# Another order for layer 2 of the first chunk: a fused attention and MLP kernel on one Trainium2 core

## The chip, the cores and the metric

The kernel runs on one core of one Trainium2 chip. The engines of the core work side by side, each through its own queue and in its own order: TensorE multiplies matrices (the profile's PE, with the loads of its stationary operand shown as PEld), VectorE (DVE) and ScalarE (ACT) work on elements, GpSimd (POOL) casts and issues DMAs, SyncE (SP) issues DMAs only. They wait for each other by semaphores. The metric is the device time of one launch in microseconds, as the median of several runs; lower is better.

## The reference

Eight batches of eight heads, 576 positions, 64 numbers a head. First attention with a causal mask and a bias from a running sum of `s`, then an MLP with the exact GELU over all 8 x 576 = 4608 tokens of width 512:

```
scores = q @ k.T / sqrt(D)
cum    = cumsum(maximum(s, 0))
scores = where(causal, -1e9, scores + minimum(-(cum_i - cum_j), 0))
attn   = softmax(scores)              # sum + 1e-9 below the line
x      = (attn @ v), heads side by side: 4608 x 512
out    = gelu(x @ w_in) @ w_out       # 512 -> 2048 -> 512
```

## The kernel before, in words

**Attention of a batch.** The kernel computes scores transposed, keys on the partitions. The bias is a product: it multiplies v by `wb`, the exponential of the running sum (`scale_v`, VectorE, one instruction for each of five key tiles of 128, the last of 64), and the row factor cancels in the division. `sc_mm(b, p, slots)` computes the scores of head pair p (0 to 3) in two units, each into one PSUM slot, and ScalarE takes the exponential of each unit into the tile P. `mask` multiplies the diagonal blocks by a triangle (VectorE). `av_main(b, qd, ...)` takes pairs qd and qd + 2: TensorE makes a denominator (`av_d`, from P and `wb`) and two products (`av_o`, from P and the scaled v, `vv`); ScalarE makes the reciprocal by a logarithm and an exponential for each half, four steps (`recip`); VectorE multiplies and writes xT, the transposed input of the MLP. `av_tails` does the same for the last 64 positions of all pairs. `squares_v` sums the squares of v on ScalarE, a 128x2048 and a 64x512 activation; the sums serve only a final test of the value range. Its output tile, `junk`, is never read.

**q and k of batches 0, 1 and 2** are loaded by GpSimd (`load_front`, cast on the way to tiles fq and fk) and transposed on TensorE (`tr_one`, one slot; `tr_two`, the banks M0 and M1), then copied to `qkT` by VectorE or ScalarE. From batch 3 on, q and k are loaded as float32 (`load_qk`), cast by GpSimd and transposed by DMA.

**The MLP** runs in nine chunks of 512 tokens; chunk c needs batch c's main part. Layer 1 has eight items (`l1_item(c, f2)`): each fills one PSUM slot with two 512-wide blocks from eight matmuls, and ScalarE takes the GELU of both at once into gT. An item must wait until the GELU of the item that used its slot before is done. Layer 2 of chunk 0 is plain: four subtiles of 128 tokens, 16 matmuls each over the 16 blocks of gT (`l2_item(c, sub, f0, f1)`), a copy to the output tile `o_sb` (one tile for two subtiles) and a store. Subtiles 0 and 1 accumulate in M0 and M1, 2 and 3 in the two halves of a slot. From chunk 1 on, layer 2 uses seven products of half-size blocks (`prod`), with sums of gT (`S`, by `sums_a`) and of w_out (`T1` to `T4`, by `sums_b`) made by VectorE.

**Stages.** While the MLP works on chunk c, the scores and products of batch c + 1 stand in between its layer-2 matmuls. The order on each engine is written out by hand: the schedule is manual, and every engine takes its instructions in the order of the calls. PSUM has eight banks: the slots x, y and z of two banks each, and the single banks M0 and M1. `order[c]` names the slots in the order in which layer 1 of chunk c takes them; for chunk 1, items 2 to 7 take s2, s1, s2, s0, s2, s0.

**Queues.** SyncE issues the loads of v (`load_v`), the stores of the output and the DMA transposes; GpSimd issues the loads of q, k and weights. Requests in a queue go in order. Some are held back by a tiny operation that reads what an earlier DMA wrote: `behind` is a small DMA on SyncE, `behind_v` a one-element copy on GpSimd that reads a tile of v. raw v of batch 1 has its buffer in common with raw k of batch 3; raw v of batches 0 and 2 share another.

ScalarE loads one set of function tables for the exponential and the logarithm (`exp_set`) and another for GELU; each switch is an ACT_TABLE_LOAD.

Of the kernel before, what the change touches and what calls it, by code (L numbers as in the profile page):

```python
# [19 lines left out]
def kernel(  # L20
# [128 lines left out]

    def behind_v(b, st):  # L150

        nc.gpsimd.tensor_copy(seen_v[:, b : b + 1], raws[b, "v"][0:1, st, 0, 0:1])

    wb = const.tile([128, ST, BH], bf16, name="wb")
    xT = work.tile([128, NP, XW], fp16, name="xT")
# [74 lines left out]
            amx[:, b * NP + p], qkT[b % 2][:, :, p, :S], axis=AX, op=ALU.max, apply_absolute_value=True  # L230
        )

    def squares_v(b):
        t = raws[b, "v"]
        n = work.tile([128, (ST - 1) * H * D], bf16, tag="P", bufs=4, name="junk")
        for j, (n_st, st0, st1) in enumerate(((128, 0, ST - 1), (SL, ST - 1, ST))):
            nc.scalar.activation(  # L237
                n[:n_st, : (st1 - st0) * H * D], t[:n_st, st0:st1].rearrange("p s h d -> p (s h d)"),
                func=AF.Square, accum_out=amv[:n_st, b, j : j + 1],
            )  # L240
# [244 lines left out]
            if lo < hi:  # L485
                yield lo, hi, (t0 + lo) % XW

    def av_pe(b, qd, den, two):

        oo = bank(two, [128, 2, 512], fp32, "av_o")  # L490
        o = [oo[:, t] for t in range(2)]
        av_mm(b, qd, den, None, MAIN)
        for t in range(2):
            av_mm(b, qd, o[t], t, MAIN)
        return o

    def av_out(b, qd, den, o):
# [7 lines left out]
                        ln[:, c * 256 + lo : c * 256 + hi], op=MULT,  # L505
                    )

    def av_main(b, qd, one, two):
        den = bank(one, [128, 512], fp32, "av_d")
        o = av_pe(b, qd, den, two)  # L510
        av_out(b, qd, den, o)

    def tails_pe(b, slot):
# [46 lines left out]
            for i in range(2):  # L560
                nc.scalar.activation(gT_of[c][:, f2 * 2 + i, :], h_ps[:, i], func=AF.Gelu)  # L561

    def l2_item(c, sub, f0=0, f1=FT, slot=None, eng=None):

        gT = gT_of[c]
        if f0 == 0:
            if slot is None:
                o_of[c, sub] = bank(M[sub % 2], [128, KO * 128], fp32, "o_ps")
            elif slot in M:
                o_of[c, sub] = bank(slot, [128, KO * 128], fp32, "o_ps")  # L570
            elif sub == 2:
                two = bank(slot, [128, 2, KO * 128], fp32, "o_ps")
                o_of[c, 2], o_of[c, 3] = two[:, 0], two[:, 1]
        o_ps = o_of[c, sub]
        for ft in range(f0, f1):
            nc.tensor.matmul(  # L576
                o_ps, lhsT=gT[:, ft, sub * 128 : (sub + 1) * 128],
                rhs=w_out_r[:, ft], start=(ft == 0), stop=(ft == FT - 1),
            )
        if f1 < FT:  # L580
            return
        if sub % 2 == 0:
            osb_of[0] = two_sb()
        copy(eng or nc.vector, osb_of[0][:, sub % 2], o_ps)
        store(c, 1 + sub // 2, osb_of[0], subs=slice(sub % 2, sub % 2 + 1))
# [315 lines left out]
    for c in range(NCH):  # L901
# [13 lines left out]
        else:  # L915
            l1_item(c, 0, 0, KO - 2)
            l1_item(c, 0, KO - 2)
            l1_item(c, 1)
        if 1 < c:
            transpose_tiles(nb)  # L920
            if nb + 1 < B:
# [6 lines left out]
        for f2 in range(2, FT // 2):  # L928
            l1_item(c, f2, slot=(s2, s1, s2, s0, s2, s0)[f2 - 2] if c == 1 else None)
            if c == 1 and f2 in (2, 4):  # L930
                tr_two(2, f2 // 2 - 1, 0, both)
                tr_one(2, f2 // 2 - 1, 1, nc.vector, (s0, s1)[f2 // 2 - 1])
            if c == 1 and f2 == 3:
                squares_v(1)
                load_qk(3, "k")
            if c == 1 and 3 <= f2 < 5:
                scale_v(2, STS[f2 - 3 : f2 - 2], nc.vector)
            if c == 1 and f2 == 5:
                sums_a(c, (1, 2, 3), 0, HF // 2)
                scale_v(2, STS[2:4], nc.vector)  # L940
                squares_v(2)
            if c > 1 and f2 == 3:
                scale_v(nb, [(0, 4), (4, 5)], nc.vector)
                sums_a(c, (1, 2, 3), 0, HF // 2)
# [7 lines left out]
                    behind(2, raws[nb + 1, "k"][0:1, ST - 2, 0, :])  # L952
                    load_v(nb + 1, [nc.sync])
        if c == 0:
            squares_v(0)
            sums_b((1, 2, 3, 4), 0, 4)
            exp_set()
            x, y, z = order[0]
            l2_item(c, 0, 0, 8)
            l2_item(c, 1, 0, 8)  # L960
            tr_one(1, 0, 0, nc.vector, z)
            tr_one(1, 0, 1, nc.scalar, x)
            l2_item(c, 2, 0, 8, y)
            sc_mm(1, 0, (z, x))
            l2_item(c, 3, 0, 8, y)
            sc_mm(1, 1, (z, x))
            mask(1, 0, nc.vector)
            sums_b((1, 2, 3), 4, 8)
            behind(1, w_out_r[0:1, FT - 5, 0:D])
            load_v(1, [nc.sync])  # L970
            l2_item(c, 0, 8, 12)
            l2_item(c, 1, 8, 12)
            tr_one(1, 1, 0, nc.vector, z)
            tr_one(1, 1, 1, nc.scalar, x)
            mask(1, 1, nc.vector)
# [250 lines left out]
```

## Time and profile before

| | us |
|---|---|
| median of 3 runs (lowest to highest) | 311.64 (311.57 to 312.32) |
| the profiled execution | 312.71 |
| its span, first to last instruction | 310.8 |
| TensorE busy | 291.5 |
| ScalarE busy | 247.1 |
| VectorE busy | 227.4 |
| GpSimd busy | 98.3 |
| mean granted TensorE clock | 0.996 of full |

The profiled execution is one of its own, beside the three timed runs. The profile gives the busy time of each engine, the chain of work that ended last (followed back from the last instruction to what released it), a timeline for each engine, and the busy time in chosen stretches. In a timeline row, the first number is the start from the beginning of the span, the second the length; then come engine, source line, operation, output and input by the program's names with shapes, and the count of instructions merged into the row. Brackets at the end give the idle time of the engine before the row and what ended it. Layer 1 of chunk 0 runs from 22.3 to 36.1, layer 2 of chunk 0 from 36.1 to 58.7, chunk 1 from 58.7 to 93.2.

### The profile page before, as it was taken

To read this page: it belongs to the slowest core of one execution; us is meant where nothing else is said; L and a number is where in the kernel's file an instruction comes from. 1 tells how busy PE (TensorE), PEld (TensorE's weight loads), DVE (VectorE), ACT (ScalarE), POOL (GpSimd) and SP (SyncE) were. 2 spreads that over 40 slices of the span, in tenths; PEclk is the share of its full clock that TensorE was granted. 3 is DMA by queue.
4 is the path that set the end of the run, shared out by engine and by line. 5 is a ranking of instruction groups with operands and counts; after the bars stand their busy time and mean duration, and the time that the engine had idled before them with its cause. 6 is when DMAs were issued, how large, how long until landed. Compare 5 with 4: busy or idle time off the path is not lost.

```text
span 310.8 us, 8463 instructions
## 1 busy us (share of the span) xinstructions
PE 291.5 (94%) x3522; PEld 196.3 (63%) x3522; DVE 227.4 (73%) x428; ACT 247.1 (80%) x348; POOL 98.3 (32%) x180
## 2 busy tenths in 40 slices
PE   0789999999999999999999999999999999999990
PEld 0564444555784578457854785478647886887880
DVE  3697347968879787787875697658797888766860
ACT  3786787879977997899788987898879877967830
POOL 6575007105080467137621953095400000000000
PEclk9999999999999999999999999999999999999998
DMA  7999999996707696969597859967990030021022
GB/s 119 195 189 203 207 179 177 278 229 149 148 15 205 120 221 135 251 114 223 116 257 142 193 116 243 199 156 152 210 223 9 2 138 2 0 96 41 2 70 76
DMA packets 77933, 45.07 MB, mean 145 GB/s; under 512 B 63168, under 2 KB 70336, under 8 KB 77888
## 3 DMA queue, kind: packets, MB, share of 16 engines
q1 hardware_dynamic: 67104, 24.93, 34.3%
q0 software_dynamic: 10784, 19.53, 32.3%
q8 instruction: 29, 0.48, 0.7%
q14 instruction: 16, 0.13, 0.1%
HBM read 36.85 MB, written 9.44 MB: 149 GB/s over the span
## 4 chain that ended last, share of the span: by engine, by line
PE 84%; ACT 6%; DVE 4%; DMA 2%; issue 2%; POOL 0%; ACTq 0%; POOLq 0%
PE h_ps L550 31%; PE o_al L764 17%; PE o_ga L764 9%; PE h_ps L667 6%; PE sc_ps L434 5%; PE o_be L764 4%; PE av_o L463 4%; ACT junk L237 3%; PE av_d L463 2%; DMA fk<-in_k_dram 2%; PE o_ps L576 2%; ACT P L440 2%; DVE vv L247 2%; PE tr_ps L395 1%; PE av_t L463 1%
## 5 line engine op out<-in xcount | busy, mean ns | idle before, releaser
L550 PE MATMUL h_ps<-xT,w_in_r 128*128 128x512 f16 x480 | 105.9, 379 | 0.4 <-ACT gT L558 0.3
L550 PEld LDWEIGHTS <-w_in_r 128*128 128x128 f16 x480 | 46.7, 98 | 54.5 <-issue 0.6
L558 ACT ACTIVATE gT<-h_ps 128x1024 f16<-128x1024 f32 x49 | 49.0, 1018 | 18.6 <-PE h_ps L550 18.5
L440 ACT ACTIVATE P<-sc_ps 128x1024 bf16<-128x1024 f32 x64 | 60.2, 1032 | 3.4 <-PE sc_ps L434 3.3
L764 PEld LDWEIGHTS <-S 128*128 128x128 f16 x512 | 48.3, 98 | 8.3 <-issue 0.9
L229 DVE TENSOR_REDUCE amx<-qkT 128x2 f32<-128x1152 bf16 x32 | 41.6, 1344 | 0.6 <-DMA qkT<-qk_bf 0.6
L764 PEld LDWEIGHTS <-gT 128*128 128x128 f16 x384 | 36.4, 98 | 7.0 <-issue 1.3
L448 DVE TENSOR_TENSOR P<-P,tri_bf 128x512 bf16<-128x512 bf16 x64 | 25.9, 419 | 11.3 <-ACT P L440 10.7
L754 DVE TENSOR_TENSOR S<-gT 128x1024 f16<-128x1024 f16 (+1 forms) x30 | 21.6, 721 | 15.1 <-ACT gT L561 13.1
L764 PE MATMUL o_al<-T,S 128*128 128x256 f16 x256 | 31.7, 273 | 0.0
L197 POOL DMA_DIRECT2D raw_k<-in_k_dram x25 | 21.0, 849 | 15.5 <-ACT junk L237 15.5
L434 PE MATMUL sc_ps<-qkT 64*128 64x256 bf16 (+2 forms) x320 | 22.3, 264 | 3.1 <-DVE qkT L404 1.7
L503 DVE TENSOR_TENSOR xT<-av_o,ln 128x256 f16<-128x256 f32 (+2 forms) x72 | 23.7, 385 | 1.7 <-ACT ln L479 1.0
L247 DVE TENSOR_TENSOR vv<-raw_v,wb 128x512 bf16<-128x512 f32 (+2 forms) x25 | 24.0, 1001 | 0.1
L434 PEld LDWEIGHTS <-qkT 64*128 64x128 bf16 x320 | 13.8, 98 | 12.2 <-issue 6.9
L197 POOL DMA_DIRECT2D raw_q<-in_q_dram x25 | 21.1, 857 | 1.2 <-POOL seen_v L148 1.2
L237 ACT ACTIVATE junk<-raw_v 128x2048 bf16<-128x2048 f32 (+1 forms) x16 | 20.3, 1266 | 0.3
L404 DVE COPY qkT<-tr_ps 128x576 bf16<-128x576 bf16 (+1 forms) x13 | 11.7, 938 | 10.4 <-PE tr_ps L395 10.4
L681 DVE TENSOR_TENSOR k<-h_ps,k 128x512 f32<-128x512 f32 (+1 forms) x12 | 11.3, 955 | 8.1 <-PE h_ps L667 5.5
L479 ACT ACTIVATE ln<-ln,lnb 128x256 f32<-128x256 f32 x32 | 16.3, 508 | 1.0
L463 PEld LDWEIGHTS <-vv 128*32 128x32 bf16 x768 | 16.3, 100 | 0.6 <-DVE vv L247 0.2
L463 PE MATMUL av_o<-P,vv 128*32 128x256 bf16 (+1 forms) x512 | 16.7, 272 | 0.0
(132 smaller groups left out, 424.9 us busy)
## 6 DMA issues: line engine op xcount, KB each, us to landing
raw_v<-in_v_dram SPq DMA_DIRECT2D x32, 256.0 KB, 5.1
out_dram<-o_sb SPq DMA_DIRECT2D x14, 512.0 KB, 3.6
raw_q<-in_q_dram POOLq DMA_DIRECT2D x20, 256.0 KB, 4.8
raw_k<-in_k_dram POOLq DMA_DIRECT2D x20, 256.0 KB, 6.9
w_out_r<-in_moe_w_out_dram POOLq DMA_DIRECT2D x4, 512.0 KB, 12.8
out_dram<-o_sb SPq DMA_DIRECT2D x7, 256.0 KB, 6.9
fq<-in_q_dram POOLq DMA_DIRECT2D x6, 288.0 KB, 6.8
fk<-in_k_dram POOLq DMA_DIRECT2D x6, 288.0 KB, 7.8
```

The lines of the kernel that those rows point to most:

```text
L197: nc.gpsimd.dma_start(out=t[:n_st, st], in_=src)
L229: nc.vector.tensor_reduce(amx[:, b * NP + p], qkT[b % 2][:, :, p, :S], axis=AX, op=ALU.max, apply_absolute_value=True)
L237: nc.scalar.activation(n[:n_st, : (st1 - st0) * H * D], t[:n_st, st0:st1].rearrange("p s h d -> p (s h d)"), func=AF.Square, accum_out=amv ...
L247: eng.tensor_tensor(vb[:n_st, st0:st1, h0:h1, :], t[:n_st, st0:st1, h0:h1, :], wb[:n_st, st0:st1, b * H + h0 : b * H + h1] .unsqueeze(3).t ...
L434: nc.tensor.matmul(s_ps[:, e, off : off + n], lhsT=qkT[b % 2][e * 64 : e * 64 + 64, 1, p, jt * 128 : jt * 128 + 128], rhs=qkT[b % 2][e * 6 ...
L440: nc.scalar.activation(P[:, :, UO[u] : UO[u] + UW[u]], s_ps[:, :, : UW[u]], func=AF.Exp, scale=scale)
L448: eng.tensor_tensor(d, d, tri_bf.unsqueeze(1).unsqueeze(1).to_broadcast([128, 2, 2, 128]), op=MULT)
L463: nc.tensor.matmul(o[g * 32 : g * 32 + 32, lo : lo + n], lhsT=(wb[:, jt, b * H + 2 * g + qd : b * H + 2 * g + qd + 1].to_broadcast([128, 3 ...
L503: nc.vector.tensor_tensor(xT[:, 2 * qd + t, x0 : x0 + hi - lo], o[t][:, c * 256 + lo : c * 256 + hi], ln[:, c * 256 + lo : c * 256 + hi], ...
L550: nc.tensor.matmul(h_ps[:, i, :], lhsT=w_in_r[:, ko, ft * 128 : (ft + 1) * 128], rhs=xT[:, ko, c * NB % XW : c * NB % XW + NB], start=(ko ...
L558: nc.scalar.activation(gT_of[c][:, f2 * 2 : f2 * 2 + 2, :], h_ps, func=AF.Gelu)
L764: nc.tensor.matmul(o[u], lhsT=lhs[:, f, u * 128 : u * 128 + 128], rhs=rhs[:, f], start=start and j == 0 and (by_sub or u == 0), stop=j == ...
```

## The change

All of it lies in chunks 0 and 1 and in batches 0, 1 and 2. The counts of matmuls, activations and bytes stay the same; seven of the eight sums of w_out of 128x1024 become fourteen of 128x512, and the copy on GpSimd is added.

- The squares of v of batch 0 move from behind layer 1 of chunk 0 to between its items 3 and 4. Those of batches 1 and 2 are cut: the 128x2048 part and the 64x512 part are issued apart, in layer 1 of chunk 1.
- In layer 2 of chunk 0, transposes, scores, masks, sums and the scaling of v of batch 1 stand at other places between the matmuls.
- In batch 1, the products come before the denominators (`last=True`).
- The last four matmuls of subtiles 2 and 3 come behind batch 1's tails, and both copies behind these; VectorE copies subtile 2, ScalarE subtile 3. Before, ScalarE copied subtile 2 and VectorE subtile 3.
- The slots of chunk 1 rotate: items 0 and 1 take z and x (before: y and z).
- v of batch 2 is requested ahead of the stores of chunk 0, and a one-element copy on GpSimd that waits for its second tile stands ahead of the request of q of batch 3.

ScalarE at the end of layer 1 of chunk 0 (gT: GELU; junk: squares; qkT: copy of the transposed k; P: exponentials), before and then after:

```order
L558 ACTIVATE gT<-h_ps 128x1024 x7
L561 ACTIVATE gT<-h_ps 128x512 x2
L237 ACTIVATE junk,amv<-raw_v 128x2048
L237 ACTIVATE junk,amv<-raw_v 64x512
L863 ACT_TABLE_LOAD
L402 COPY qkT_119<-tr_ps 128x2x576
```

```order
L558 ACTIVATE gT<-h_ps 128x1024 x4
L238 ACTIVATE junk,amv<-raw_v 128x2048
L238 ACTIVATE junk,amv<-raw_v 64x512
L558 ACTIVATE gT<-h_ps 128x1024 x3
L561 ACTIVATE gT<-h_ps 128x512 x2
L866 ACT_TABLE_LOAD
L403 COPY qkT_119<-tr_ps 128x2x576
```

The two squares moved from ahead of the table load to behind the fourth GELU.

ScalarE from the tails of batch 1 (lnt) into layer 1 of chunk 1, before and then after:

```order
L479 ACTIVATE lnt<-lnt,lnb 128x128
L558 ACT_TABLE_LOAD
L558 ACTIVATE gT<-h_ps 128x1024 x4
L237 ACTIVATE junk,amv<-raw_v 128x2048
L237 ACTIVATE junk,amv<-raw_v 64x512
L558 ACTIVATE gT<-h_ps 128x1024 x2
```

```order
L480 ACTIVATE lnt<-lnt,lnb 128x128
L403 COPY o_sb<-o_ps 128x512
L558 ACT_TABLE_LOAD
L558 ACTIVATE gT<-h_ps 128x1024 x2
L238 ACTIVATE junk,amv<-raw_v 128x2048
L558 ACTIVATE gT<-h_ps 128x1024 x2
L238 ACTIVATE junk,amv<-raw_v 64x512
L558 ACTIVATE gT<-h_ps 128x1024
```

An output copy came in ahead of the table load, and the large square moved up from behind the fourth GELU to behind the second.

SyncE's requests (raw_v: v of batches 1, 2 and 3; out_dram: stores of chunk 0), before and then after:

```order
L225 DMA raw_v<-in_v_dram 128x8x64 x4
L225 DMA raw_v<-in_v_dram 64x8x64
L779 DMA out_dram<-o_sb 128x512 x4
L225 DMA raw_v<-in_v_dram 128x8x64 x4
L225 DMA raw_v<-in_v_dram 64x8x64
```

```order
L225 DMA raw_v<-in_v_dram 128x8x64 x4
L225 DMA raw_v<-in_v_dram 64x8x64
L225 DMA raw_v<-in_v_dram 128x8x64 x4
L225 DMA raw_v<-in_v_dram 64x8x64
L782 DMA out_dram<-o_sb 128x512 x4
```

The four stores moved behind the five loads of v of batch 2.

```diff
-    def squares_v(b):
+    def squares_v(b, js=(0, 1)):
         t = raws[b, "v"]
         n = work.tile([128, (ST - 1) * H * D], bf16, tag="P", bufs=4, name="junk")
-        for j, (n_st, st0, st1) in enumerate(((128, 0, ST - 1), (SL, ST - 1, ST))):
+        for j in js:
+            n_st, st0, st1 = ((128, 0, ST - 1), (SL, ST - 1, ST))[j]
...
-    def av_pe(b, qd, den, two):
+    def av_pe(b, qd, den, two, last=False):
...
-        av_mm(b, qd, den, None, MAIN)
-        for t in range(2):
-            av_mm(b, qd, o[t], t, MAIN)
+        for t in (0, 1, None) if last else (None, 0, 1):
+            av_mm(b, qd, den if t is None else o[t], t, MAIN)
...
-    def l2_item(c, sub, f0=0, f1=FT, slot=None, eng=None):
+    def l2_item(c, sub, f0=0, f1=FT, slot=None, eng=None, out=True):
...
-        if f1 < FT:
-            return
+        if f1 == FT and out:
+            l2_out(c, sub, eng)
+
+    def l2_out(c, sub, eng=None):
+        o_ps = o_of[c, sub]
         if sub % 2 == 0:
             osb_of[0] = two_sb()
         copy(eng or nc.vector, osb_of[0][:, sub % 2], o_ps)
...
+        if c == 1:
+            squares_v(1, (0,))
...
+            if c == 0 and f2 == 3:
+                squares_v(0)
+                sums_b((1, 2, 3, 4), 0, 2)
             if c == 1 and f2 == 3:
-                squares_v(1)
+                squares_v(1, (1,))
                 load_qk(3, "k")
...
+            if c == 1 and f2 == 4:
+                squares_v(2, (0,))
             if c == 1 and f2 == 5:
                 sums_a(c, (1, 2, 3), 0, HF // 2)
                 scale_v(2, STS[2:4], nc.vector)
-                squares_v(2)
+                sums_b((4,), 4, 8)
+                squares_v(2, (1,))
...
         if c == 0:
-            squares_v(0)
-            sums_b((1, 2, 3, 4), 0, 4)
+            sums_b((1, 2, 3, 4), 2, 4)
             exp_set()
             x, y, z = order[0]
             l2_item(c, 0, 0, 8)
-            l2_item(c, 1, 0, 8)
             tr_one(1, 0, 0, nc.vector, z)
             tr_one(1, 0, 1, nc.scalar, x)
+            l2_item(c, 1, 0, 8)
+            sc_mm(1, 0, (z, x))
             l2_item(c, 2, 0, 8, y)
-            sc_mm(1, 0, (z, x))
+            mask(1, 0, nc.vector)
+            sc_mm(1, 1, (z, x))
             l2_item(c, 3, 0, 8, y)
-            sc_mm(1, 1, (z, x))
-            mask(1, 0, nc.vector)
-            sums_b((1, 2, 3), 4, 8)
+            sums_b((1, 2, 3), 4, 6)
             behind(1, w_out_r[0:1, FT - 5, 0:D])
             load_v(1, [nc.sync])
+            tr_one(1, 1, 0, nc.vector, z)
+            tr_one(1, 1, 1, nc.scalar, x)
             l2_item(c, 0, 8, 12)
             l2_item(c, 1, 8, 12)
-            tr_one(1, 1, 0, nc.vector, z)
-            tr_one(1, 1, 1, nc.scalar, x)
             mask(1, 1, nc.vector)
-            sums_b((4,), 4, 8)
             behind_v(1, 1)
             for qd in range(2):
                 for n in "qk":
                     load_front(2, n, qd)
+            sc_mm(1, 2, (z, x))
+            sums_b((1, 2, 3), 6, 8)
+            scale_v(1, STS[0:2], nc.vector)
             l2_item(c, 2, 8, 12)
             l2_item(c, 3, 8, 12)
-            sc_mm(1, 2, (z, x))
-            l2_item(c, 0, 12, eng=nc.scalar)
+            mask(1, 2, nc.vector)
             sc_mm(1, 3, (z, x))
-            mask(1, 2, nc.vector)
-            scale_v(1, STS, nc.vector)
-            l2_item(c, 1, 12, eng=nc.scalar)
-            l2_item(c, 2, 12, eng=nc.scalar)
+            load_v(2, [nc.sync])
+            scale_v(1, STS[2:5], nc.vector)
+            for i in range(2):
+                l2_item(c, i, 12, eng=nc.scalar)
             mask(1, 3, nc.vector)
-            av_main(1, 0, M[0], z)
-            l2_item(c, 3, 12)
-            av_main(1, 1, M[1], x)
+            av_main(1, 0, M[0], z, last=True)
+            av_main(1, 1, M[1], x, last=True)
             av_tails(1, M[0])
-            order[1] = (y, z, x)
-            load_v(2, [nc.sync])
+            l2_item(c, 2, 12, out=False)
+            l2_item(c, 3, 12, out=False)
+            l2_out(c, 2)
+            l2_out(c, 3, nc.scalar)
+            order[1] = (z, x, y)
+            behind_v(2, 1)
             load_qk(3, "q")
```

More of the change, by code (lines that the diff above doesn't have):

```diff
@@ L150, in behind_v @@
     def behind_v(b, st):
-        nc.gpsimd.tensor_copy(seen_v[:, b : b + 1], raws[b, "v"][0:1, st, 0, 0:1])
+        nc.gpsimd.tensor_copy(seen_v[:, b % 2 : b % 2 + 1], raws[b, "v"][0:1, st, 0, 0:1])
     wb = const.tile([128, ST, BH], bf16, name="wb")
@@ L506, in av_out, with av_main @@
                     )
-    def av_main(b, qd, one, two):
+    def av_main(b, qd, one, two, last=False):
         den = bank(one, [128, 512], fp32, "av_d")
-        o = av_pe(b, qd, den, two)
+        o = av_pe(b, qd, den, two, last)
         av_out(b, qd, den, o)
```

## The prediction

> **What bounds it now.** I read the page first, then the chain of work that ended last, then the stretches of the span around the change.
>
> ```profile
> span 310.8 us, 8463 instructions
> ...
> PE 84%; ACT 6%; DVE 4%; DMA 2%; issue 2%; POOL 0%; ACTq 0%; POOLq 0%
> ```
>
> The chain is TensorE for 84% of the span. So a microsecond that TensorE stops waiting is worth a microsecond, as long as nothing later hands it back. What there is to win is seen by comparing a stretch with a quiet one of the same work. Columns: stretch, its length, busy us (and instructions) of TensorE, weight load, VectorE, ScalarE and GpSimd, then clock, DMA share and GB/s.
>
> ```profile
> 36.10:58.70 22.60, 21.79 (x393) 11.41 (x392) 14.00 (x30) 19.05 (x27) 7.22 (x10) 1.00 1.06 192
> 58.70:74.75 16.05, 15.70 (x209) 7.52 (x208) 13.37 (x20) 13.35 (x20) 3.87 (x5) 1.00 0.80 214
> 74.75:83.05 8.30, 7.88 (x89) 5.95 (x88) 5.99 (x13) 8.27 (x11) 0.35 (x1) 1.00 0.72 153
> 93.20:107.00 13.80, 13.80 (x66) 6.26 (x64) 12.94 (x12) 11.26 (x14) 1.82 (x5) 1.00 0.65 160
> 107.00:114.87 7.87, 7.87 (x89) 6.02 (x88) 5.02 (x11) 7.84 (x10) 7.04 (x9) 1.00 0.94 212
> ```
>
> The first row is layer 2 of chunk 0, the second layer 1 of chunk 1, the third the start of its layer 2. The last two are the same two stages of chunk 2, where TensorE has no gap (13.80 and 7.87 busy of as much). The third row is 0.43 longer than the fifth (8.30 - 7.87). The rows of TensorE around the change, with the idle time of the engine and what ended it in brackets:
>
> ```profile
> 40.38 1.90 PE L576 MATMUL o_ps<-w_out_r,gT 128*128 128x512 f16 x8
> 42.51 0.61 PE L434 MATMUL sc_ps<-qkT 64*128 64x256 bf16 x10 [0.23 <-ACT qkT L402]
> 43.06 1.90 PE L576 MATMUL o_ps<-w_out_r,gT 128*128 128x512 f16 x8
> 44.89 0.61 PE L434 MATMUL sc_ps<-qkT 64*128 64x256 bf16 x10
> 45.44 1.90 PE L576 MATMUL o_ps<-w_out_r,gT 128*128 128x512 f16 x8
> ...
> 51.47 0.39 PE L434 MATMUL sc_ps<-qkT 64*128 64x256 bf16 x4
> 52.37 0.40 PE L434 MATMUL sc_ps<-qkT 64*128 64x256 bf16 x6 [0.52 <-ACT P L440]
> ...
> 54.53 0.57 PE L463 MATMUL av_d<-P,wb 128*32 128x256 bf16 x16
> 54.93 1.07 PE L463 MATMUL av_o<-P,vv 128*32 128x256 bf16 x32
> ...
> 57.29 0.94 PE L463 MATMUL av_o<-P,vv 128*32 128x256 bf16 x32
> ...
> 58.70 5.34 PE L550 MATMUL h_ps<-xT,w_in_r 128*128 128x512 f16 x24
> ...
> 64.05 0.76 PE tr_ps L395 x72
> ...
> 71.30 3.61 PE L550 MATMUL h_ps<-xT,w_in_r 128*128 128x512 f16 x16 [0.34 <-ACT gT L558]
> ...
> 80.89 0.40 PE L434 MATMUL sc_ps<-qkT 64*128 64x256 bf16 x6 [0.42 <-ACT P L440]
> ```
>
> Ends are modelled, so I measure from start to start. Eight layer-2 matmuls take 1.83 (43.06 to 44.89), ten score matmuls 0.55 (44.89 to 45.44). Hence four places lose time: 0.30 at 42.51 (due at 42.21), 0.68 at 52.37 (four of ten take 0.22, due at 51.69), 0.13 in the attention product (1.07 against 0.94; it waits for scaled v), and in layer 1 of chunk 1, where the 13.80 of chunk 2 plus two transpose groups of 0.76 would make 15.32, 0.73.
>
> **The change, part by part.** The rows of ScalarE and VectorE from which I price it:
>
> ```profile
> 37.27 1.91 ACT L237 ACTIVATE junk<-raw_v 128x2048 bf16<-128x2048 f32 x1
> ...
> 40.05 1.28 ACT L863 ACT_TABLE_LOAD   x1
> 41.34 1.12 ACT L402 COPY qkT<-tr_ps 128x1152 bf16<-128x1152 bf16 x1
> ...
> 52.83 3.09 DVE L247 TENSOR_TENSOR vv<-raw_v,wb 128x512 bf16<-128x512 f32 x5
> ...
> 57.52 0.39 ACT L478 ACTIVATE ln<-av_d 128x256 f32<-128x256 f32 x1 [0.26 <-PE av_d L463]
> ...
> 57.98 0.68 DVE L404 COPY o_sb<-o_ps 128x512 f32<-128x512 f32 x1
> ...
> 59.16 0.26 ACT L478 ACTIVATE lnt<-av_t 128x128 f32<-128x128 f32 x1
> ...
> 59.87 1.28 ACT L558 ACT_TABLE_LOAD   x1
> ...
> 59.96 0.41 DVE L524 TENSOR_TENSOR xT<-av_t,lnt 128x256 f16<-128x256 f32 x1
> ...
> 67.59 1.90 ACT L237 ACTIVATE junk<-raw_v 128x2048 bf16<-128x2048 f32 x1
> ...
> 69.62 0.63 ACT L237 ACTIVATE junk<-raw_v 64x512 bf16<-64x512 f32 x1
> ...
> 77.98 7.44 ACT L440 ACTIVATE P<-sc_ps 128x1024 bf16<-128x1024 f32 x8
> ...
> 94.15 1.28 ACT L558 ACT_TABLE_LOAD   x1
> 95.44 1.02 ACT L558 ACTIVATE gT<-h_ps 128x1024 f16<-128x1024 f32 x1
> ...
> 109.78 7.46 ACT L440 ACTIVATE P<-sc_ps 128x1024 bf16<-128x1024 f32 x8
> ```
>
> *Squares of v, batch 0.* They hold ScalarE from 37.27 to 40.05 (2.78), ahead of the table load and the k copy (41.34 to 42.46) for which the scores wait at 42.51. Now they stand between the GELUs of items 3 and 4 of layer 1, where ScalarE (13.80 long, 11.26 busy in chunk 2's row) has room. A GELU of 1024 elements takes 0.93 (7.46 / 8), an item 1.73 (13.80 / 8). So the slack is 0.80 an item, and 2.78 is worked off over items 4 to 7. GELU 4 ends about 1.0 + 2.78 + 0.93 = 4.7 after item 3; item 7, which needs its bank, begins 3 x 1.73 = 5.2 after it. Hence nothing; the cover is 0.5. The k copy comes 2.5 earlier: -0.30.
>
> *Scores and layer 2 interleaved.* The scores of head pair 3 now follow those of pair 2 with eight matmuls (1.83) between instead of four; the two activations need 2 x 0.93 plus a start some 0.4 into them, and the first bank is free after one. -0.68. The first two tiles of v are scaled earlier, which leaves 3.09 x 3/5 behind the mask: -0.13. The sums of w_out are only cut in halves; VectorE is busy 14.00 of 22.60 there, so an added 0.3 of starts is covered.
>
> *Products before denominators.* The logarithms start later, and the tail's bank is freed by the third of four activations (57.52 to 59.16: 0.41 each, so 1.23). TensorE has about 1.2 of work meanwhile (a denominator of 0.40, from 54.53 to 54.93, and products of 0.94 with their drain). With a hand-over each way I take +0.25, between 0 and 0.5. Chunk 0: -0.30 - 0.68 - 0.13 + 0.25 = -0.86, **-0.9**. Layer 1 of chunk 1 then starts at t0 = 57.8 instead of 58.70.
>
> *The last two subtiles.* Their eight matmuls (1.83) now stand between the tails and t0, so layer 1 finds xT ready. But the copies moved behind the tails' result. Sub 3 goes to ScalarE, behind VectorE's copy of sub 2 into the same output tile. From t0: the second four logarithm steps end about -0.4, the tail pair 0.71 later (59.16 to 59.87) at +0.3, VectorE's tail product (0.41) and copy (0.68) at +1.4, ScalarE's copy (I take VectorE's 0.68) at +2.1, the table load (1.28) at +3.4, two GELUs at +5.2. Then stands the *128x2048 square of batch 1's v*, 2.03 with its read (67.59 to 69.62): +7.2, and GELU 2 ends at +8.2. TensorE wants GELU 2's bank for item 4 at t0 + 4 x 1.73 + 0.76 = +7.7. So a new wait of about **0.55** at item 4. It replaces the 0.73 above: -0.2. The rest of the squares (0.72; batch 2's 2.03 and 0.72) fit behind GELUs 3, 4 and 5: counted on, GELU 7 ends 1.1 after layer 2 begins, and the exponentials start 2.4 after it. Before, that was 3.23 (74.75 to 77.98), in chunk 2, without a wait, 2.78 (107.00 to 109.78). So the wait at 80.89 goes: **-0.43**.
>
> *Table loads against the skill.* At 94.15 the load took 1.28 and the first GELU began at 95.44; nothing else is paid. The Trainium skill ("ScalarE: Activation LUTs", What ACT_TABLE_LOAD costs) gives about 1.28 us for the load as well, but adds a drain of about 1.38 us to each switch; by it the wait at item 4 would be 1.93, and the time 1.38 above my forecast for that switch alone. This trace does not show the drain, so I keep 1.28.
>
> *DMA.* On SP, v of batch 2 is requested straight behind v of batch 1 and ahead of four stores; on GpSimd, a one-element copy waits for its second tile before q of batch 3 is requested. The transfers that could now be late are the k and q of batch 2 (and v of batch 1):
>
> ```profile
> L106 POOL DMA_DIRECT2D fk<-in_k_dram x2: 700/704/707, 49.1 to 50.4; - x2
> ...
> DMA to landing us min/median/max: 5.6/6.9/8.2
> ...
> L225 SPq DMA_DIRECT2D raw_v<-in_v_dram x5: 582/924/1602, 42.5 to 46.6; - x5
> ...
> DMA to landing us min/median/max: 4.2/4.2/4.2
> ```
>
> The k's land at 54.7 and 58.6 (issue plus 5.6 and 8.2); they are needed after items 2 and 4, at t0 + 3 x 1.73 = 63.0 and about 67.8. The five loads of v of batch 1 took from 42.5 to 50.8 (the last one's issue at 46.6 plus its own 4.2): 8.3. If as much went wholly ahead of the k's, they would land at 63.0 and 66.9. So: nothing, with 0 to 0.1 as bounds. The earlier request itself wins nothing: no row above waits for v of batch 2. The stores have only the next chunk's output tiles behind them, some 20 us later, and q of batch 3 is not cast until batch 2's masks are done.
>
> **The sum**: -0.9 - 0.2 - 0.43 = -1.5. The profiled execution took 312.71 (310.8 of span and 1.9 around it) and would take 311.2; the median of the runs is 311.64, 1.07 less, and I forecast **310.1** there. A change under 0.3% (0.93) is about what cannot be told from none.
>
> **Rivals.**
>
> (a) *Every wait is covered*: GELU 2 comes in time, because ScalarE's copy does not wait for VectorE's or the tail steps run faster. For it speaks that only 0.55 is missing; against, that the copies share a tile. Then 0.55 and 0.25 more go: 309.3.
>
> (b) *VectorE holds the attention product*: the scaling of v's first two tiles now stands ahead of pair 2's mask, so a late v delays both. The products begin at about t0 - 5.0 = 52.8, and two tiles (0.62 each) are still to be scaled behind that mask, so they must have landed by 51.6. For: the last tile landed at 50.8, and the new requests share the transfers' engines. Against: they stand behind it in the same queue. Each microsecond beyond costs one. With 1 us: 311.1, no change.
>
> (c) *Slower: k of batch 2 is late.* It decides from 63.0 on. To end above 312.6 the wait must exceed the gain of 1.5 and the 0.93, so the k must land at 65.4, 10.7 later than now. The bound above is 8.3. Time then: 312.8 and more.
>
> (d) *ScalarE's two moved switches cost a second 1.28 each.* The wait at item 4 grows to 1.83 and the exponentials start 3.7 after layer 2's begin, 0.9 over chunk 2's: 1.28 and about 0.9 on my forecast, 312.3. The rows at 94.15 speak against. It is the mechanism that the Trainium skill's drain would make here.
>
> (e) *The gain is given back later*, by a transfer of batch 3 that does not move with TensorE: 311.6. Against: from 83 us on everything is released by TensorE or what follows it.
>
> **Numbers.** Chances: forecast 0.52 (309.6 to 310.6), (a) 0.17, (b) 0.13, (c) 0.06, (d) 0.04, (e) 0.05, others 0.03. The range reaches down past (a) and up through (b): 309.1 to 311.2, which leaves out about 0.18. Faster by over 0.3% (below 310.7): forecast, (a), a fifth of (b), 0.72. Same: most of (b), (d) and (e), 0.19. Slower: (c), a part of (d) and others, 0.09.
>
> **What would show it.** Right: the scores of batch 1 without an idle bracket; layer 1 of chunk 1 beginning at about 57.8; an idle bracket of about 0.5 there at item 4, released by a GELU of L558, with ScalarE idle for about 1 us ahead of its output copy; the first exponential some 2.4 after layer 2's first product. Wrong: an idle bracket released by DMA at the transposes of batch 2, by VectorE's vv at the products, or a longer one at item 4 or 7; a GELU that starts long after its table load; or gaps beyond 90 us, where there are none now.

## The result and the profile after

The changed kernel takes **309.96 us** (median of eight runs, 309.57 to 311.02), the kernel before 312.12 beside it (eight runs, 311.57 to 312.61): a ratio of **0.9941, 95% interval 0.9924 to 0.9958**. That is 2.16 us less; the forecast was 310.1, and 1.5 less. The page of the changed kernel begins so; its profiled execution took 309.57.

```profile
span 307.7 us, 8472 instructions
```

The forecast of the time came closer than that of the difference: it started from the 311.64 of three runs, and the kernel before gave 312.12 in eight. The span fell by 3.1 us, twice the forecast, so the first question is where. The same stages as in the prediction, in the changed kernel (stretch, length, busy us and instructions of TensorE, weight load, VectorE, ScalarE, GpSimd, then clock, DMA share, GB/s):

```profile
22.30:36.19 13.89, 13.89 (x67) 6.29 (x65) 9.37 (x16) 11.28 (x14) 4.59 (x7) 0.99 1.19 206
36.19:57.51 21.32, 21.17 (x394) 11.46 (x393) 13.65 (x32) 16.66 (x24) 3.07 (x5) 1.00 1.15 197
57.51:73.60 16.09, 15.70 (x209) 7.52 (x208) 12.79 (x18) 13.90 (x19) 8.63 (x11) 1.00 0.98 245
73.60:81.47 7.87, 7.80 (x89) 6.01 (x87) 7.16 (x16) 7.54 (x9) 0.00 (x0) 1.00 0.52 112
81.47:91.61 10.14, 10.14 (x212) 8.81 (x209) 7.63 (x24) 8.33 (x16) 6.23 (x17) 1.00 0.38 64
```

And VectorE's last instruction, before and then after:

```profile
303.36 0.43 DVE L404 COPY o_sb<-o_al 128x256 f32<-128x256 f32 x1 [1.05 <-PE o_al L764]
```

```profile
301.80 0.42 DVE L405 COPY o_sb<-o_al 128x256 f32<-128x256 f32 x1 [1.05 <-PE o_al L767]
```

| stage | before | after | difference | forecast |
|---|---|---|---|---|
| layer 1 of chunk 0 | 13.80 | 13.89 | +0.09 | 0 |
| layer 2 of chunk 0 | 22.60 | 21.32 | **-1.28** | -0.86 |
| layer 1 of chunk 1 | 16.05 | 16.09 | **+0.04** | -0.2 |
| its layer 2, up to o_ga | 8.30 | 7.87 | -0.43 | -0.43 |
| the rest of chunk 1 | 10.14 | 10.14 | 0 | 0 |
| chunk 2 to the last copy | 210.17 | 210.19 | +0.02 | 0 |
| last copy to the end of the span | 7.44 | 5.90 | -1.54 | 0 |

(For before, the last two rows go from 93.19 to 303.36 and on to 310.8; for after from 91.61 to 301.80 and on to 307.7.) The work itself ends 1.56 earlier. The other 1.54 lies behind the last copy, in the last stores and the end of the program, which the change does not touch; the same stretch took 6.3 to 7.1 in eleven further executions (span less the start of the last copy), and 6.3 and 6.7 in two of the same kernel (e1 and e8 below). The profile of before had a long end and that of after a short one, and I take that part as scatter. Nor is the +0.09 in layer 1 of chunk 0 a cost of the squares: the granted clock in that stretch was 0.99 against 1.00 before, and nine of the eleven further profiles, all with the squares of batch 0 at the new place, took 13.81 to 13.83 there.

TensorE's rows around the change, after it:

```profile
40.58 0.61 PE L435 MATMUL sc_ps<-qkT 64*128 64x256 bf16 x10
...
50.28 0.61 PE L435 MATMUL sc_ps<-qkT 64*128 64x256 bf16 x10
...
52.66 0.95 PE L464 MATMUL av_o<-P,vv 128*32 128x256 bf16 x32
53.43 0.56 PE L464 MATMUL av_d<-P,wb 128*32 128x256 bf16 x16
...
54.58 0.56 PE L464 MATMUL av_d<-P,wb 128*32 128x256 bf16 x16
55.29 0.30 PE L464 MATMUL av_t<-P,wb 128*32 128x64 bf16 x16
55.40 0.44 PE L464 MATMUL av_t<-P,vv 128*32 128x64 bf16 x32
55.77 1.90 PE L576 MATMUL o_ps<-w_out_r,gT 128*128 128x512 f16 x8
57.51 5.34 PE L550 MATMUL h_ps<-xT,w_in_r 128*128 128x512 f16 x24
...
63.54 1.90 PE L550 MATMUL h_ps<-xT,w_in_r 128*128 128x512 f16 x8
65.83 1.89 PE L550 MATMUL h_ps<-xT,w_in_r 128*128 128x512 f16 x8 [0.39 <-ACT gT L558]
```

All score groups start without an idle bracket, the products take their 0.77, and one wait is left with a bracket: item 4, 2.29 behind item 3 instead of 1.73. From 54.58 to 55.29 stands 0.71 for a denominator of 0.39, so the tails wait 0.32 (too little for a bracket behind modelled ends). ScalarE beside it:

```profile
59.15 0.58 ACT L403 COPY o_sb<-o_ps 128x512 f32<-128x512 f32 x1 [1.15 <-DVE o_sb L405]
59.75 1.28 ACT L558 ACT_TABLE_LOAD   x1
61.04 1.94 ACT L558 ACTIVATE gT<-h_ps 128x1024 f16<-128x1024 f32 x2
62.87 1.91 ACT L238 ACTIVATE junk<-raw_v 128x2048 bf16<-128x2048 f32 x1
...
64.76 1.94 ACT L558 ACTIVATE gT<-h_ps 128x1024 f16<-128x1024 f32 x2
...
76.20 3.98 ACT L441 ACTIVATE P<-sc_ps 128x1024 bf16<-128x1024 f32 x4
```

This is the sequence that the prediction worked out: idle 1.15 ahead of the output copy, the table load, two GELUs, the large square, and GELU 2 only at 64.76.

One view misleads here. The chain of work that ended last has, in the changed kernel, TensorE at 75% instead of 84%, and steps onto a load of v of batch 2:

```profile
55.72 6.26 DMA raw_v<-in_v_dram
61.98 1.00 ACT gT L558
```

But ScalarE has no idle time ahead of 61.98: the second GELU follows the first, begun at 61.04, by 0.94, and the square follows that. The chain names what signalled last, and a load happened to land then. The square reads v of batch 1, not of batch 2, and the first experiment shows that it does not wait for that load.

### The profile page after: what moved, and what is told of

Its sections match the earlier page's. It is cut to its first block, busy times and chain, and to the rows that moved or that the text cites. A ratio compares the mean times of both kernels' runs of the same rounds, so it can differ in the third digit from the quotient of the medians.

```text
span 307.7 us, 8472 instructions
## 1 busy us (share of the span) xinstructions
PE 290.6 (94%) x3522; PEld 196.4 (64%) x3522; DVE 228.0 (74%) x435; ACT 246.9 (80%) x348; POOL 98.3 (32%) x181
## 3 DMA queue, kind: packets, MB, share of 16 engines
HBM read 36.85 MB, written 9.44 MB: 150 GB/s over the span
## 4 chain that ended last, share of the span: by engine, by line
PE 75%; DMA 9%; issue 7%; SPq 3%; ACT 2%; POOL 1%; DVE 1%; POOLq 0%
PE h_ps L550 27%; PE o_al L767 18%; PE o_ga L767 9%; PE h_ps L670 6%; PE o_be L767 5%; PE sc_ps L435 4%; DMA raw_v<-in_v_dram 4%; DMA w_in_r<-in_moe_w_in_dram 4%; PE av_o L464 3%; SPq L225 3%; PE av_d L464 2%; DMA fq<-in_q_dram 1%; PE av_t L464 1%; ACT gT L558 1%; ACT junk L238 1%
## 5 line engine op out<-in xcount | busy, mean ns | idle before, releaser
L435 PE MATMUL sc_ps<-qkT 64*128 64x256 bf16 (+2 forms) x320 | 21.4, 257 | 2.3 <-DVE qkT L405 1.8
```

Of the source, the lines that this page charges most:

```text
L435: nc.tensor.matmul(s_ps[:, e, off : off + n], lhsT=qkT[b % 2][e * 64 : e * 64 + 64, 1, p, jt * 128 : jt * 128 + 128], rhs=qkT[b % 2][e * 6 ...
```

## The experiments

The start of layer 2 of chunk 0 lies anywhere from 35.73 to 37.09 in the profiles (layer 1 of chunk 0 itself began anywhere from 21.61 to 23.15; what moves it was not looked into), so below I count from there (its first matmul, L576). The expectations give moments of the span; where the start had moved, the difference to it is what counts. Columns: that start; then, counted from it, layer 1 of chunk 1, its layer 2, o_ga (the first matmul into that tile, which follows the scores of batch 2), and the last copy; then the ratio to the kernel before with its interval, where it was timed.

| kernel | start | layer 1 | layer 2 | o_ga | last copy | ratio |
|---|---|---|---|---|---|---|
| before | 36.10 | 22.60 | 38.65 | 46.95 | 267.26 | |
| after | 36.19 | 21.32 | 37.41 | 45.28 | 265.61 | 0.9941 (0.9924-0.9958) |
| e1 copy on VectorE | 36.06 | 21.32 | 36.86 | 44.73 | 265.04 | |
| e2 denominators first | 36.46 | 21.60 | 37.24 | 45.11 | 265.42 | |
| e3 e1 and e2 | 36.33 | 21.60 | 37.14 | 45.01 | 265.32 | 0.9944 (0.9925-0.9963) |
| e4 v of batch 2 late | 35.73 | 21.31 | 38.52 | 46.39 | 266.78 | 0.9963 (0.9941-0.9984) |
| e5 squares back | 36.48 | 21.32 | 37.36 | 45.66 | 265.98 | |
| e6 before, squares of batch 0 moved | 36.04 | 22.19 | 38.23 | 46.53 | 266.85 | 0.9984 (0.9966-1.0001) |
| e7 four matmuls between | 35.76 | 22.01 | 38.10 | 45.97 | 266.28 | |
| e8 as e1, timed | 36.85 | 21.32 | 36.86 | 44.73 | 265.05 | 0.9926 (0.9909-0.9943) |
| e9 e1 and tails between | 37.09 | 21.21 | 36.76 | 44.63 | 264.95 | 0.9919 (0.9903-0.9935) |
| e10 e4, squares of batch 2 back | 36.08 | 21.31 | 37.42 | 46.08 | 266.47 | |
| e11 e4 and e5 | 36.62 | 21.31 | 37.35 | 45.66 | 266.04 | |

**What makes GELU 2 late: the output copy (e1).**

```diff
-            l2_out(c, 3, nc.scalar)
+            l2_out(c, 3)
```

> The changed kernel, with the last output copy of chunk 0 (subtile 3) on VectorE instead of ScalarE. Theory (late GELU 2 because ScalarE's copy waits 1.15 us for VectorE's): the idle time ahead of that copy goes, the table load stands straight behind the tail's logarithms at about 58.0, GELU 2 ends at about 64.9 and item 4 of layer 1 of chunk 1 starts on time, at 65.3 instead of 65.83. Layer 2 of chunk 1 then begins at 73.05 instead of 73.60 and the last instruction of VectorE starts at 301.25 instead of 301.80 (-0.55). Rival (the large square of v alone makes GELU 2 late): item 4 still waits 0.4 or more, and VectorE's last instruction stays within 0.15 of 301.80.

TensorE, then ScalarE, then the loads of v in a stretch of it (the view by tile):

```profile
63.41 3.63 PE L550 MATMUL h_ps<-xT,w_in_r 128*128 128x512 f16 x16
...
72.92 1.91 PE L767 MATMUL o_al<-w_out_r,gT 128*128 128x256 f16 x16
```

```profile
57.89 1.28 ACT L558 ACT_TABLE_LOAD   x1
60.17 1.94 ACT L558 ACTIVATE gT<-h_ps 128x1024 f16<-128x1024 f32 x2 [0.99 <-PE h_ps L550]
61.99 1.91 ACT L238 ACTIVATE junk<-raw_v 128x2048 bf16<-128x2048 f32 x1
```

```profile
L225 SPq DMA_DIRECT2D raw_v<-in_v_dram x2: 4080/4266/4453, 51.9 to 56.4; - x2
...
DMA to landing us min/median/max: 6.4/8.4/10.4
```

Items 3 and 4 are one row of sixteen matmuls again, the load stands straight behind the tail's logarithms, and layer 2 begins 0.55 earlier, as the theory said to the hundredth. The square still stands ahead of GELU 2; without the late copy it does no harm. The edit takes two things off ScalarE, the copy's wait of 1.15 and the copy's own 0.58, so the table load comes 1.73 earlier (0.51 instead of 2.24 behind the start of layer 1); e1 does not tell the two apart. The square begins at 61.99, while the last loads of v of batch 2 land at 62.3 and 62.8 (51.9 + 10.4, 56.4 + 6.4): it did not wait for them, and the chain's step onto raw_v above was no dependence.

**Is that kept to the end (e8)?** The same kernel, timed.

> The changed kernel with subtile 3's copy on VectorE, timed. Theory: it keeps the 0.55 that its profile showed from the start of layer 2 of chunk 0 to layer 2 of chunk 1 (36.86 instead of 37.41), so the median is 0.5 below the changed kernel's 309.96, at about 309.4, a ratio of 0.992 to the kernel before. Rival: the 0.55 is given back behind chunk 1 (a later transfer, or the last stores), and the median is at 310.

The last copy starts 265.05 behind the start of layer 2, against 265.04 in e1's profile and 265.61 in the changed kernel: kept. The median is 309.92 (309.04 to 310.43, six runs), which is the rival's number and not the theory's. The ratio, 0.9926 against 0.9941, is lower, but the intervals overlap: the runs scatter too much for half a microsecond, and the verdict rests on the profile.

**What carries layer 1 and the start of layer 2 of chunk 1: the squares of batches 1 and 2 (e5).**

```diff
-        if c == 1:
-            squares_v(1, (0,))
...
             if c == 1 and f2 == 3:
-                squares_v(1, (1,))
+                squares_v(1)
...
-            if c == 1 and f2 == 4:
-                squares_v(2, (0,))
...
-                squares_v(2, (1,))
+                squares_v(2)
```

> The changed kernel, with the squares of v of batches 1 and 2 whole behind items 3 and 5 of layer 1 of chunk 1, as before the change. Theory (the place of the squares decides which wait there is): no wait at item 4; a wait of 0.3 to 0.5 at item 6, whose bank GELU 4 frees behind 2.8 of squares; layer 1 as long as now (16.1); GELU 7 late, so the first exponential starts 3.2 after layer 2's first product instead of 2.6, and a wait of 0.4 stands among the scores of layer 2. VectorE's last instruction at 302.2 instead of 301.80. Rival (the wait at item 4 comes from the copy and the table load, not from the square): item 4 still waits 0.3 or more.

```profile
70.39 3.61 PE L550 MATMUL h_ps<-xT,w_in_r 128*128 128x512 f16 x16 [0.34 <-ACT gT L558]
...
79.98 0.40 PE L435 MATMUL sc_ps<-qkT 64*128 64x256 bf16 x6 [0.41 <-ACT P L441]
```

The wait at item 4 goes, the one of the kernel before at item 6 is back, layer 1 is as long as ever (16.04), and layer 2 waits 0.41 for an exponential, as before the change. All of the 0.43 there is the squares' place; in layer 1 they only choose which item waits, as long as ScalarE's copy is late. The wait at item 4 thus needs both, the late copy and the square ahead of GELU 2: it goes with either (e1, e5).

**What the early request of v is worth (e4, e10, e11).**

```diff
-            load_v(2, [nc.sync])
             scale_v(1, STS[2:5], nc.vector)
...
-            behind_v(2, 1)
+            load_v(2, [nc.sync])
             load_qk(3, "q")
```

> The changed kernel, with the loads of v of batch 2 requested behind the four stores of chunk 0 again, and without the one-element copy on GpSimd. Theory (the early request is worth nothing, since nothing waits for v of batch 2, and q and k of batch 3 have time): layer 1 of chunk 1 at 57.5, layer 2 of chunk 1 at 73.6, VectorE's last instruction within 0.1 of 301.80, median 310. Rival (the order of the requests is part of the gain, by fewer transfers beside the k's of batch 2, or of the loss): one of these moments moves by 0.3 or more, with an idle bracket of TensorE or VectorE released by a DMA.

```profile
69.57 1.91 ACT L238 ACTIVATE junk<-raw_v 128x2048 bf16<-128x2048 f32 x1 [1.25 <-DMA raw_v<-in_v_dram]
```

```profile
72.53 1.89 PE L550 MATMUL h_ps<-xT,w_in_r 128*128 128x512 f16 x8 [0.91 <-ACT gT L558]
```

The theory, which was also the prediction's step, falls. The square of batch 2 now waits 1.25 for v, GELU 5 stands behind it, and item 7 waits 0.91 for GELU 5's bank: layer 2 begins 1.11 later. In the kernel before, these squares came at 72.06, late enough for v. To see whether the request is worth something without the moved squares, e10 moves only those of batch 2 back (the diff, on top of e4's), e11 those of both batches (e4's diff and e5's).

```diff
-            if c == 1 and f2 == 4:
-                squares_v(2, (0,))
...
-                squares_v(2, (1,))
+                squares_v(2)
```

> The kernel with v of batch 2 requested behind the stores, and the squares of batch 2 whole behind item 5 again too. Theory (the early request is needed only because the squares of batch 2 were moved up; alone it is worth nothing): ScalarE no longer waits 1.25 for raw v ahead of the square, item 7 no longer waits 0.91, layer 2 of chunk 1 begins 37.4 behind the start of layer 2 of chunk 0 (38.52 with the early squares, 37.41 in the changed kernel), and the wait of 0.4 among its scores returns, so that o_ga starts 45.7 behind instead of 46.39. Rival (late v of batch 2 costs by itself, in the scaled v or the attention product): layer 2 of chunk 1 still begins 38 or more behind.

> The kernel with the squares of batches 1 and 2 back behind items 3 and 5, and v of batch 2 requested behind the stores as well. Theory (with the squares at their old places the early request is worth nothing): all of chunk 1 as in the kernel that moved only the squares back: from the start of layer 2 of chunk 0, layer 2 of chunk 1 begins at 37.36 and its o_ga at 45.66, both within 0.1. Rival (late v of batch 2 costs by itself, through the scaled v for which VectorE waited 0.59 in the last kernel): one of these two is later by 0.3 or more, with TensorE or ScalarE released by VectorE's vv or by a DMA.

e10, and then e11, both TensorE:

```profile
65.73 1.89 PE L550 MATMUL h_ps<-xT,w_in_r 128*128 128x512 f16 x8 [0.41 <-ACT gT L558]
...
73.50 2.25 PE L767 MATMUL o_al<-w_out_r,gT 128*128 128x256 f16 x16
...
80.00 0.40 PE L435 MATMUL sc_ps<-qkT 64*128 64x256 bf16 x6 [0.44 <-ACT P L441]
```

```profile
70.52 3.61 PE L550 MATMUL h_ps<-xT,w_in_r 128*128 128x512 f16 x16 [0.34 <-ACT gT L558]
...
80.11 0.40 PE L435 MATMUL sc_ps<-qkT 64*128 64x256 bf16 x6 [0.41 <-ACT P L441]
```

In e10 item 7's wait is gone and layer 2 begins at 37.42, as expected; o_ga came at 46.08, not 45.7. The other 0.34 is a wait that I had not counted: the first product of layer 2 takes 2.25 instead of 1.91, I think since it needs the last GELU, which stands behind the squares of batch 2 (that GELU begins 1.22 behind the product here, 0.86 in e5 and 0.20 in the changed kernel), while layer 1 was held up at item 4 and not, as in e5, at item 6. e11 is clean: with all squares at their old places, late v gives the same times as early v (37.35 and 45.66, against e5's 37.36 and 45.66). So the early request is worth nothing by itself, and 1.1 us once the squares are moved up. The two edits are one.

**The parts of chunk 0 (e6, e7).** e6 is the kernel before with the squares of batch 0 moved alone:

```diff
+            if c == 0 and f2 == 3:
+                squares_v(0)
...
-            squares_v(0)
             sums_b((1, 2, 3, 4), 0, 4)
```

> The kernel before, with one part of the change alone: the squares of v of batch 0 between items 3 and 4 of layer 1 of chunk 0. Theory (they delay the copy of k for which the first scores wait): the idle time ahead of the scores at 42.5 goes, layer 2 of chunk 0 takes 22.3 instead of 22.60, everything behind it moves up by 0.3, and VectorE's last instruction starts at 303.06 instead of 303.36. Layer 1 of chunk 0 keeps its 13.80 to 13.9. Rival (the exponentials of the later pairs set the pace): the wait at 42.5 goes, but the later wait for the exponentials grows by as much, and layer 2 still takes 22.5 or more.

```profile
42.16 0.61 PE L434 MATMUL sc_ps<-qkT 64*128 64x256 bf16 x10
...
51.90 0.40 PE L434 MATMUL sc_ps<-qkT 64*128 64x256 bf16 x6 [0.52 <-ACT P L440]
```

The wait ahead of the first scores is gone, and the later one for the exponential is no longer than it was (0.52): layer 2 takes 22.19, 0.41 less. That is 0.3 at these scores and 0.1 more at the second pair of transposes (0.85 before, from 47.27 to 48.12; 0.73 here, from 46.91 to 47.64). In e7, four of the eight matmuls ahead of the last scores go behind them:

```diff
             l2_item(c, 2, 8, 12)
-            l2_item(c, 3, 8, 12)
             mask(1, 2, nc.vector)
             sc_mm(1, 3, (z, x))
+            l2_item(c, 3, 8, 12)
```

> The changed kernel, with four layer-2 matmuls instead of eight between the scores of head pairs 2 and 3 (the other four behind pair 3). Theory (pair 3's scores need the banks whose exponentials take 0.93 each): the scores of pair 3 wait 0.7 again, released by an exponential, and layer 1 of chunk 1 begins at 58.2 instead of 57.51. Rival (the exponentials now run ahead, since the copy of k is not late any more): no wait over 0.2 at those scores, and layer 1 begins by 57.7.

```profile
48.98 0.39 PE L435 MATMUL sc_ps<-qkT 64*128 64x256 bf16 x4
49.89 0.40 PE L435 MATMUL sc_ps<-qkT 64*128 64x256 bf16 x6 [0.52 <-ACT P L441]
```

The old wait returns with its old bracket, and layer 1 begins 0.69 later (22.01 against 21.32): the prediction's 0.68.

**The tails' wait (e2, e3, e9).** e2 puts the denominators ahead of the products again; e3 is e1 and e2 together.

```diff
-            av_main(1, 0, M[0], z, last=True)
-            av_main(1, 1, M[1], x, last=True)
+            av_main(1, 0, M[0], z)
+            av_main(1, 1, M[1], x)
```

> The changed kernel, with the denominators of batch 1 ahead of the products again. Theory (the tails wait 0.32 for the logarithms that read M0): the tails start right behind the last product, layer 1 of chunk 1 begins at 57.2 instead of 57.51, item 4 waits as long as now, and VectorE's last instruction starts at 301.5 instead of 301.80. Rival (ScalarE is held by the two output copies until 53.7 in any case, so its logarithms cannot start earlier): the tails keep 0.2 to 0.3 of their wait and the start of layer 1 stays within 0.15 of 57.51.

> Both edits of the two kernels ahead: subtile 3 copied on VectorE and denominators first. Theory (two separate waits): the gains add up, -0.55 and -0.3; VectorE's last instruction starts at 300.95, and the median is about 309.1. Rival (with layer 1 starting earlier, GELU 2 is again what ends last, because the tails' logarithms and VectorE's work do not come earlier): 0.3 of the wait at item 4 returns, and the last instruction starts at about 301.25, as with the copy alone.

TensorE in e2, and then ScalarE:

```profile
51.10 1.90 PE L576 MATMUL o_ps<-w_out_r,gT 128*128 128x512 f16 x8
53.51 0.57 PE L464 MATMUL av_d<-P,wb 128*32 128x256 bf16 x16 [0.52 <-ACT o_sb L403]
...
55.81 0.30 PE L464 MATMUL av_t<-P,wb 128*32 128x64 bf16 x16
...
58.06 5.34 PE L550 MATMUL h_ps<-xT,w_in_r 128*128 128x512 f16 x24
...
64.09 3.72 PE L550 MATMUL h_ps<-xT,w_in_r 128*128 128x512 f16 x16
```

```profile
52.87 1.08 ACT L403 COPY o_sb<-o_ps 128x512 f32<-128x512 f32 x2
```

For the start of layer 1, neither theory nor rival. The tails no longer wait, but the denominator does, 0.58 (eight matmuls begun at 51.10 end at 52.93): it needs M0, which still holds subtile 0 of layer 2 until ScalarE has copied it. Layer 1 begins 0.28 later, not 0.3 earlier. Yet e2 as a whole is 0.19 ahead of the changed kernel (last copy at 265.42 instead of 265.61). Counted from the start of layer 2 of chunk 0, ScalarE's table load comes 0.18 earlier than in the changed kernel (23.38 instead of 23.56), so item 4, which waits for ScalarE, comes earlier too: items 3 and 4 take 3.66 together (64.09 to 67.75), so the wait there is about 0.1 instead of 0.56. With e1's copy on VectorE nothing waits at item 4, the later start of layer 1 counts in full, and the two gains do not add: e3 is 0.28 worse than e1, and its median 310.49, where the theory had 309.1. What the order "products first" hides in chunk 0 is this bank, but in the changed kernel layer 1 hands back more than that.

e9 keeps the products first, takes e1's copy, and lets four matmuls cover the tails' wait:

```diff
-            av_tails(1, M[0])
             l2_item(c, 2, 12, out=False)
+            av_tails(1, M[0])
             l2_item(c, 3, 12, out=False)
             l2_out(c, 2)
-            l2_out(c, 3, nc.scalar)
+            l2_out(c, 3)
```

> As the kernel ahead, and the tails of batch 1 behind the last four matmuls of subtile 2 instead of ahead of them. Theory (the tails wait 0.32 for the second logarithm that reads M0, and four matmuls of 0.87 cover that): the wait ahead of the tails goes, layer 1 of chunk 1 begins 21.0 behind the start of layer 2 of chunk 0 instead of 21.32, layer 2 of chunk 1 36.55 behind it instead of 36.86, and the median is about 309.1. Rival (layer 1 then waits for VectorE's products, which end 0.6 behind its present start): layer 1's first items lose the 0.3 again, and layer 2 of chunk 1 stays at 36.86.

```profile
55.48 0.56 PE L464 MATMUL av_d<-P,wb 128*32 128x256 bf16 x16
55.97 1.04 PE L576 MATMUL o_ps<-w_out_r,gT 128*128 128x512 f16 x4
56.94 0.30 PE L464 MATMUL av_t<-P,wb 128*32 128x64 bf16 x16
...
57.43 1.04 PE L576 MATMUL o_ps<-w_out_r,gT 128*128 128x512 f16 x4
58.30 5.34 PE L550 MATMUL h_ps<-xT,w_in_r 128*128 128x512 f16 x24
```

The wait of 0.32 is gone, but only 0.10 is won, and not because layer 1 waited, as the rival had it (layer 2 begins 15.55 behind layer 1, as in e8's 15.54). The change-overs eat it: the first group of four takes 0.97 until the tails start, the second, which runs into matmuls of its own kind, 0.87, and the denominator ahead of them 0.49 where 0.39 was usual. In these rows each extra change between kinds of matmul costs about 0.1. By the timed runs (0.9919), e9 cannot be told from e8 or from the changed kernel, whose intervals overlap with its own; by the profile it is the best, 0.66 ahead of the changed kernel.

## Why the prediction was right, point by point

The time (310.1 for 309.96) and the sign came out, and the sum, -1.5, is what the work shows (-1.56). But several terms were off and made up for each other (chunk 0 won 0.42 more than forecast, layer 1 of chunk 1 0.24 less), so that the sum came so close is partly luck. So is the 310.1: with the 312.12 of the eight runs in place of the 311.64 of three, the same sum would have given 310.6.

- *Squares of batch 0, -0.30*: cause right; it measures -0.41 (e6), since a wait of 0.1 at the second transposes went with it.
- *Scores with eight matmuls between, -0.68*: right (e7: 0.69).
- *Products held by scaled v, -0.13*: mis-sized. I took the difference of modelled lengths (1.07 and 0.94). From start to start the product took 1.00 (54.93 to 55.93) against 0.77 (57.29 to 58.06): 0.23. "I measure from start to start" was my own rule.
- *Tails wait for the logarithms, +0.25*: right, 0.32. But I put it down as the price of the order, against an order that waits for nothing: with denominators first, they would wait 0.58 for M0 (e2), and layer 1 would begin 0.28 later. I had not asked what M0 held. Nor had I followed the order into layer 1: in the changed kernel denominators first would have ended 0.19 earlier, since item 4 then waits less; only with the copy on VectorE do the products belong first (e3 against e1).
- *Not priced at all*: from the tails' start to the next work passed 0.64 before (58.06 to 58.70) and 0.48 after (55.29 to 55.77); and the 64 layer-2 matmuls, their waits left out, took 14.65 before and 14.55 after, since two groups of four were joined, one of sixteen was split, and the last eight now run into matmuls of their own kind. With these 0.16 and 0.10, the terms add up: -0.41 - 0.69 - 0.23 + 0.32 - 0.16 - 0.10 = -1.27, and chunk 0 gained 1.28 instead of 0.86.
- *Item 4 of layer 1, a wait of 0.55*: right in place, releaser and size (2.29 - 1.73 = 0.56; idle ahead of the copy 1.15, forecast about 1). e1 and e5 show its two causes, the late copy and the square; how much of the lateness the copy's wait for VectorE makes, and how much the copy itself, they do not separate.
- *"It replaces the 0.73 above: -0.2"*: this step failed. The 0.73 was not one wait. 0.52 stood at item 6; the other 0.2 is two hand-overs into the transposes of about 0.1, and these are there in every version (e1, where no item waits, takes 15.54, 0.22 over the 15.32 of the prediction). 0.56 for 0.52 is no gain (+0.04).
- *The wait in layer 2 of chunk 1, -0.43*: right (7.87; e5 brings it back). The first exponential came 2.60 behind layer 2's first product, forecast 2.4.
- *DMA, "the earlier request itself wins nothing: no row above waits for v of batch 2"*: the step that failed most. I looked for a wait in the trace of before, where the squares still stood late. Moved up, they need the early request (e4: 1.11 lost). The forecast held because I had priced the squares with v at hand, and the change brings both.
- *Nothing given back later*: right, 210.19 for 210.17.

The rivals. (a): the waits of 0.56 and 0.32 are there. (b): the products took their 0.77. (c): no idle bracket at the transposes of batch 2. (d): the GELU begins at 61.04, straight behind a table load of 1.28 begun at 59.75. The Trainium skill ("ScalarE: Activation LUTs", What ACT_TABLE_LOAD costs) adds a drain of about 1.38 to each switch; by it the wait at item 4 would be some 1.9, an estimate from the page's figure, and it is 0.56. The trace does not agree with it. (e): see above.

As to the medians: they differ by 2.16, the work by 1.56. The interval of the ratio reaches from 1.3 to 2.4 us, so both fit. For the kernels that were timed, the difference of the last column by itself (1.65, 1.94, 0.48, 0.41, 2.21 and 2.31 for after, e3, e4, e6, e8 and e9) lies in the interval each time but for e4, whose 0.48 is just outside (0.5 to 1.8).

## What to carry to other kernels

Price edits that are made together as one: before writing "nothing waits for this transfer", look for who will want it earlier once the other edits are in. Before adding up the excess of a stage as a wait to be won, take it apart into waits with a releaser and the hand-overs that every version pays. And when two instructions change places, ask of the bank that each of them takes who still reads it. An earlier start of a stage is worth only what the next wait leaves of it: follow the order to that wait before pricing it.

## What was not expected of the hardware

- On SP, the issuing of a load took longer when many stood ahead of it. With v of both batches requested in a row, the ten issues took 17.15 us, 0.58 the first and 4.3 each of the last two, and the four stores behind them began at 60.15, though the tiles of the first two had been copied by 53.7:

```profile
42.88 17.15 SPq L225 DMA_DIRECT2D raw_v<-in_v_dram x10
60.15 2.10 SPq L782 DMA_DIRECT2D out_dram<-o_sb  x4
```

  In e4 five loads were issued in 4.40 and the stores from 52.76. Why the issues grew longer no run here shows. I had put the stores off by the order alone. Here nothing needed their buffers, and it cost nothing.
- The middle of the program repeats to the hundredth (265.04 and 265.05 for e1 and e8, the same kernel and the only such pair), while its two ends move: the start of layer 2 of chunk 0 over 1.36 us, the stretch from the last copy to the end of the span over 1.5, in thirteen profiles. Half a microsecond is seen in one profile between fixed points, and hardly in a median of eight.
